# Experts in three blocks, then the second net; x operands in two sets; decode over two blocks

## The chip, the cores and the metric

The program runs on one core of one Trainium2 chip. The metric is the device time of one execution in microseconds; lower is better. Of several executions the median is given.

## The reference, cut to what matters

Three stages follow each other, on 2304 tokens with 512 features, in float32.

```python
# 1. attention inside chunks of 64 tokens, 4 x 8 heads, head size 64
attn = softmax(q_c @ k_c.T / sqrt(64)); x = attn @ v_c           # -> (2304, 512)
# 2. eight experts with weights P from 8 Sinkhorn rounds
P = exp(x @ w_gate - max)
for _ in range(8):
    P /= P.sum(1, keepdims=True) + 1e-9
    P /= P.sum(0, keepdims=True) + 1e-9
    P *= N / E
y = sum(P[:, e:e+1] * (relu(x @ w1[e]) @ w2[e]) for e in range(8))  # 512 -> 1024 -> 512
# 3. the second net: three products, their maximum, one product
h = maximum(maximum(y @ u1, y @ u2), y @ u3)                        # 512 -> 768
out = h @ w_out                                                     # 768 -> 512
```

Stage 3 for a token needs y of that token alone, so a block of tokens can pass to stage 3 as soon as all eight experts are summed for it.

## The kernel before, in words

The tokens are cut into three blocks of 768. A phase is one stage on one block: ("M", b) runs the experts on block b, ("m", b) the second net. An expert phase has 32 items (8 experts, 4 pairs of 128 hidden features each), a phase of the net has 9 (3 pairs of features, 3 products for the maximum). Items are numbered through: before, 0 to 31 and 32 to 63 are the experts on blocks 0 and 1, 64 to 72 the net on block 0, 73 to 104 the experts on block 2, 105 to 113 and 114 to 122 the net on blocks 1 and 2.

An item's up half (`up`, L187) is a Strassen scheme of seven products, so that 7 products replace 8. Each operand is kept as a high and a low part (`xh`, `xl` for x, `wh`, `wl` for weights), and each product is six matmuls of 384 columns on TensorE (L235). Between products ScalarE copies a partial sum out of PSUM (`s`, L240), VectorE adds (L243), and `finish` (L208) makes the hidden operands `hh` and `hl`; in the net it takes the maximum into `m` (L225) first. The down half (`down`, L256) is six matmuls of 512 columns per tile of 128 tokens (L267), six tiles per expert item and six per three items of the net. The down tiles of an item are placed between the products of the following items: after products 0 to 5 of an expert item, or after products 2 and 4 of an item of the net.

The order of the work is written out by hand. The main loop (L712) walks the items and their seven products; `at(n, pos, fn)` (L606) hangs other work behind product `pos` of item `n`. Each engine runs its instructions in that order. All transfers are issued from SP's queue, in that order too.

What hangs there:

- Weights of an item are made in block 0 (`prep`), kept in device memory (`keep`, tensors `w1s`, `w2s`), and loaded again for later blocks: `fetch(n + 1)` behind product 1, `fetch2(n)` at product 2, before the work hung there (L725).
- `y_out` (L305) transposes the summed outputs of an expert phase tile by tile early in the next phase and stores them (`ys`).
- The weights of the second net come as 64-bit floats and are decoded on the chip by `decode_all` (L410): 24 jobs of eight or nine steps, two loads ahead, with integer operations on VectorE, a high part on ScalarE (`dhi`), a low part on POOL (`dlo`), and two stores to `scr` or `scro`. The first step of the next job (L388) writes `scm`, which has the same buffer as `dhi`, and stands in one step with the stores. The steps hang on the second block of experts (L641).
- The x operands of a phase are changed at its start. `x_load` (L329) reads them four and three items ahead, `x_sums` (L339) makes the Strassen differences two items ahead, and `x_put` (L345) writes `xh` and `xl`, one of seven parts behind each product of the last item before the phase, since the matmuls of that item still read them. In the first phase, `x_head` (L349) makes them from the attention in pieces of 128 columns instead.

SBUF tiles come from pools; `big` (opened by `att_close`, L627) holds `m`, the decode's buffers and the tiles of `x_load`.

Of the kernel before, what the change touches and what calls it, by code (L numbers as in the profile page):

```python
# [9 lines left out]
F32 = mybir.dt.float32  # L10
F32R = mybir.dt.float32r
# [7 lines left out]
P = 128  # L19
# [10 lines left out]
KD = DM // P  # L30
SB = 3
TS = NT // SB
W = TS * P // 2
NPAIR = E * F // 256
# [3 lines left out]
NPE = 6  # L38
# [9 lines left out]
def kernel(ctx: ExitStack, tc: tile.TileContext, qk, vv, wg, wts, wts2, out):  # L48
    nc = tc.nc
    pool = lambda name, bufs=1, **kw: ctx.enter_context(tc.tile_pool(name=name, bufs=bufs, **kw))  # L50
    cp = pool("const")
    wp = pool("w", 2)
    hp_ = pool("h", 2)
    tp_ = pool("t", 1)
    raws = ExitStack()
    rp = raws.enter_context(tc.tile_pool(name="raw", bufs=1, side="right"))
    accp = pool("acc")
# [12 lines left out]
    mr = cp.tile([1, P], F32, name="mr")  # L70
    rs = cp.tile([P, NT], F32, name="rs")
    cs = cp.tile([P, E], F32, name="cs")
    cp.tile([P, 480], F32, name="gap")
    xh = cp.tile([P, 7, 2, W], F32R, name="xh")
    xl = cp.tile([P, 7, 2, W], F32R, name="xl")
    xs = dram.tile([NT, P, KD, P], F32, name="xs")
    ys = dram.tile([NT, P, KD, P], F32, name="ys")
# [5 lines left out]
    wts2 = wts2.bitcast(I32)  # L83


    phases = [("M", 0), ("M", 1), ("m", 0), ("M", 2), ("m", 1), ("m", 2)]
    items, first_of = [], []
    for kind, sb in phases:
        first_of.append(len(items))
# [11 lines left out]
    st, sw, wh, wl, w2h, w2l = {}, {}, {}, {}, {}, {}  # L101
# [85 lines left out]
    def up(n):  # L187
        it = items[n]
        bank = {"a": ps_a.tile([P, 512], F32, name="pa", tag="pa"),
                "g": ps_g.tile([P, 512], F32, name="pg", tag="pg"),  # L190
                "b": ps_b.tile([P, 512], F32, name="pb", tag="pb")}
        bank = {k: t[:, :W] for k, t in bank.items()}
        begun = set()
        tiny = lambda nm: tp_.tile([P, W], F32, name=nm, tag=nm)
        m2 = it["kind"] == "m"
        if not m2:
            c = tp_.tile([P, 3, W], F32, name="c", tag="c")
        elif it["i"] == 0:
            mt[0] = big[0].tile([P, 4, W], F32, name="m", tag="big")
            c = mt[0]  # L200
        else:
            c = tp_.tile([P, 3, W], F32, name="c", tag="c")
        if it["down"]:
            hh = hp_.tile([P, 4, W], F32R, name="hh", tag="hh")
            hl = hp_.tile([P, 4, W], F32R, name="hl", tag="hl")
            it["h"] = (hh, hl)

        def finish(q, src):  # L208

            if not m2:  # L210
                nc.scalar.activation(out=hh[:, q], in_=src, func=AF.Relu)  # L211
                if q.start == 0:
                    nc.scalar.activation(out=src, in_=src, func=AF.Relu)  # L213
                    nc.gpsimd.tensor_tensor(out=hl[:, q], in0=src, in1=hh[:, q].bitcast(F32),  # L214
                                            op=ALU.subtract)
                    return
                nc.vector.scalar_tensor_tensor(out=hl[:, q], in0=src, scalar=0.0,  # L217
                                               in1=hh[:, q].bitcast(F32), op0=ALU.max, op1=ALU.subtract)
                return
            m = mt[0]  # L220
            if it["i"] == 0:
                if q.start == 3:
                    nc.scalar.copy(out=m[:, q], in_=src)
                return
            nc.vector.tensor_tensor(out=m[:, q], in0=src, in1=m[:, q], op=ALU.max)  # L225
            if it["i"] == 2:
                hilo(hh[:, q], hl[:, q], m[:, q])

        s = {}
        for pos, (wi, xi, b) in enumerate(PRODUCTS):  # L230
            ps = bank[b]
            for k in range(2):
                ws = slice(k * P, (k + 1) * P)
                for i, (x, y) in enumerate(((wh[n], xh), (wh[n], xl), (wl[n], xh))):
                    nc.tensor.matmul(ps, lhsT=x[:, wi, ws], rhs=y[:, xi, k], start=b not in begun,  # L235
                                     stop=k == 1 and i == 2, skip_group_check=True)
                    begun.add(b)
            if pos < 3:
                s[pos] = tiny(f"s{pos}")
                nc.scalar.copy(out=s[pos], in_=ps)  # L240
            elif pos < 6:
                q, other = {3: (0, 0), 4: (1, 1), 5: (2, 2)}[pos]
                nc.vector.tensor_tensor(out=c[:, q], in0=ps, in1=s[other], op=ALU.add)  # L243
                if pos == 4:
                    finish(slice(0, 2), c[:, 0:2])
                elif pos == 5:
                    finish(slice(2, 3), c[:, 2:3])
            else:
                finish(slice(3, 4), ps.unsqueeze(1))
            yield pos  # L250
# [94 lines left out]
    def x_put(pos):  # L345
        i = PRODUCTS[pos][1]
        hilo(xh[:, i], xl[:, i], xst[i], nc.vector if pos % 2 == 0 else None)

    def x_head(j, r, eng):  # L349

        cols = slice(j * P, (j + 1) * P)
        T = ap_.tile([P, 4, 2, P], F32, name="xT", tag="xT", bufs=1)
        for o, a, b in ((T[:, 0], r[:, 1, 0:2], r[:, 0, 0:2]), (T[:, 1], r[:, 1, 2:4], T[:, 0]),
                        (T[:, 2], r[:, 1, 2:4], r[:, 1, 0:2]), (T[:, 3], r[:, 0, 2:4], T[:, 1])):
            eng.tensor_tensor(out=o, in0=a, in1=b, op=ALU.subtract)
        yield
        raw = r[:, 0].rearrange("p (i k) q -> p i k q", i=2)
        nc.scalar.copy(out=xh[:, 0:2, :, cols], in_=raw)
        nc.scalar.copy(out=xh[:, 2, :, cols], in_=r[:, 1, 2:4])
        nc.gpsimd.tensor_tensor(out=xl[:, 0:2, :, cols], in0=raw, in1=xh[:, 0:2, :, cols].bitcast(F32),  # L360
                                op=ALU.subtract)
        nc.gpsimd.tensor_tensor(out=xl[:, 2, :, cols], in0=r[:, 1, 2:4], in1=xh[:, 2, :, cols].bitcast(F32),
                                op=ALU.subtract)
        for i in range(2):
            c = slice(3 + 2 * i, 5 + 2 * i)
            nc.scalar.copy(out=xh[:, c, :, cols], in_=T[:, 2 * i:2 * i + 2])
        yield
        for i in range(2):
            c = slice(3 + 2 * i, 5 + 2 * i)
            nc.vector.tensor_tensor(out=xl[:, c, :, cols], in0=T[:, 2 * i:2 * i + 2],  # L370
                                    in1=xh[:, c, :, cols].bitcast(F32), op=ALU.subtract)
        yield


    big = [None]

    def decode_load(srcs):
        w = big[0].tile([P, 512, 2], I32, name="w64", tag="ld", bufs=3)
# [72 lines left out]
    ap_ = att.enter_context(tc.tile_pool(name="att", bufs=2))  # L451
    wones = ap_.tile([P, 2 * DM], BF16, name="wones", tag="eT", bufs=1)[:, 0:DM]
    q_t, v_t, s_t, e_t, et_t, at_t, raw_t = {}, {}, {}, {}, {}, {}, {}
# [152 lines left out]
    def at(n, pos, fn):  # L606
        bg.setdefault((n, pos), []).append(fn)
# [18 lines left out]

    def att_close():  # L627
        att.close()
        big[0] = pool("big")

    def raw_close():
        raws.close()
# [5 lines left out]
        for step in range(4):  # L638
            at(g + step // 3, (0, 1, 6, 1)[step], lambda g=g, step=step: keep(g, step))
    dec, folds = decode_all(), fold_all()  # L640
    for a in range(NPAIR + 1, first_of[2] - 1):  # L641
        for b in range(7):
            for _ in range(1 + (b == 3)):
                at(a, b, lambda: next(dec, None))
    at(first_of[2] - 2, 6, lambda: [None for _ in dec])
    f0 = 4 * NRAW + 2
    for i in range(NRAW * TS + 2):
        at(f0 + i // 4, (0, 2, 4, 5)[i % 4], lambda: next(folds, None))
    for k in range(1, len(phases)):
        n0 = first_of[k]  # L650
        g = x_load(k)
        for i in range(13):
            at(n0 - 4 + i // 7, i % 7, lambda g=g: next(g, None))
        for step in range(4):
            at(n0 - 2, step + 2, lambda step=step: x_sums(step))
        for pos in range(7):
            at(n0 - 1, pos, lambda pos=pos: x_put(pos))

    def warm(n):
        p = wk.tile([P, 512], F32, name="warm", tag="wk")  # L660
# [3 lines left out]
    with tc.manual_schedule():  # L664
# [14 lines left out]
        for k in range(NPE + 2):  # L679
            if k < NPE:  # L680
                att_qk(k)
                load_qk(k + 3)
            if k >= 2:
                att_pv(k - 2)
                load_v(k + 1)
            if 1 <= k <= NPE:
                att_norm(k - 1)
            if k < NPE:
                att_exp(k, 2)
            if 1 <= k <= NPE:  # L690
                att_T(k - 1)
            warm(4 if k < NPE else 0)
            if k == 0:
                prep(0, 0)
                raw1(1)
            if k == 1:
                prep(0, 1)
            if k == 3:
                prep(0, 2)
                raw2(1)  # L700
            if xg:
                next(xg.pop(0))
            if k >= 3 and k % 2:
                g = x_head(k // 2 - 1, raw_t[k // 2 - 1], nc.gpsimd if k < NPE else nc.vector)
                next(g)
                next(g)
                xg.append(g)
# [72 lines left out]
```

## Time and profile before

| | us |
|---|---|
| median of 3 runs | 1940.75 (1938.32 to 1941.76) |
| the profiled execution | 1934.4 |
| its span, first to last instruction | 1932.6 |
| TensorE busy with matmuls | 1882.9 |
| VectorE (DVE) busy | 1116.0 |
| ScalarE (ACT) busy | 690.7 |
| GpSimd (POOL) busy | 636.1 |
| mean granted TensorE clock | 0.989 of full speed |

Durations are from one profiled execution, on its own clock. Starts in the trace are counted from the first instruction. The busy times are sums over the span, and matmuls overlap, so a full TensorE row does not tell how close to its best it runs; the times between like places of successive items do. The chain of waits is followed back from the last instruction, and successive matmuls of one destination are one piece in it, with their number behind an x.

### The profile page before, as it was taken

Reading aid. Unit: us, or ns where it says so; the run is one execution under the profiler, and the core shown is the slowest. Engines: PE = TensorE matmul, PEld = TensorE weight load, DVE = VectorE, ACT = ScalarE, POOL = GpSimd, SP = SyncE. Lnnn points to the kernel's source line nnn. Section 1 sums busy time; section 2 is a strip of 40 time slices with the busy share of each in tenths; the row PEclk is TensorE's granted clock in tenths of the full one; section 3 lists DMA queues with packets and bytes.
Section 4 is the critical chain, followed back from the end, with each engine's and each line's share of the span. In section 5 each row is a group of like instructions: output and inputs, shape, how many; then the busy total and the mean of one; then the engine's idle time right before and its main releaser. Section 6 shows DMA issues by size and latency. Waiting matters only on the chain.

```text
span 1932.6 us, 26875 instructions
## 1 busy us (share of the span) xinstructions
PE 1882.9 (97%) x10397; PEld 1681.6 (87%) x10403; DVE 1116.0 (58%) x1748; ACT 690.7 (36%) x1194; POOL 636.1 (33%) x438
## 2 busy tenths in 40 slices
PE   7999999999999999999999999999999999999998
PEld 4988888888888888889888989898989988889897
DVE  7566555637875777677766545444445444453534
ACT  4545554454444333233323332322222222233221
POOL 6666666778872221222221211211111111111201
PEclk8999999999999999999999999999999999999999
DMA  7587967778888766767776457544444444647562
GB/s 252 189 301 265 329 248 278 284 278 297 328 325 300 255 228 235 269 240 253 264 264 226 188 214 259 212 180 179 180 180 180 182 189 191 225 172 253 192 247 93
DMA packets 172673, 455.30 MB, mean 236 GB/s; under 512 B 14465, under 2 KB 81025, under 8 KB 172545
## 3 DMA queue, kind: packets, MB, share of 16 engines
q1 hardware_dynamic: 172544, 453.58, 64.1%
q8 instruction: 82, 1.34, 0.3%
q14 instruction: 47, 0.38, 0.1%
HBM read 319.57 MB, written 132.38 MB: 234 GB/s over the span
## 4 chain that ended last, share of the span: by engine, by line
PE 88%; DVE 4%; DMA 4%; ACT 3%; issue 1%; POOL 1%; SPq 0%; DVEq 0%; ACTq 0%; POOLq 0%
PE dn L267 42%; PE pa L235 24%; PE pg L235 12%; PE pb L235 6%; DMA w2l<-w2s 2%; DMA scr<-dhi 1%; PE s L478 1%; PE gp L569 1%; DVE c L243 1%; PE warm L662 1%; ACT hh L211 1%; PE xp L557 1%; DVE acc L290 1%; DVE xl L182 1%; DVE hl L217 0%
## 5 line engine op out<-in xcount | busy, mean ns | idle before, releaser
L267 PE MATMUL dn<-w2h,hh 128*128 128x512 f32 x1260 | 498.9, 396 | 12.3 <-ACT hh L181 6.0
L267 PE MATMUL dn<-w2h,hl 128*128 128x512 f32 x1260 | 502.8, 399 | 3.7 <-DVE hl L217 3.4
L267 PE MATMUL dn<-w2l,hh 128*128 128x512 f32 x1260 | 499.8, 397 | 2.8 <-DMA w2l<-w2s 2.8
L290 DVE SCALAR_TENSOR_TENSOR acc<-dn,Pt,acc 128x512 f32<-128x512 f32 x438 | 327.1, 747 | 276.2 <-PE dn L267 274.8
L214 POOL TENSOR_TENSOR hl<-c,hh 128x768 fp32r<-128x768 f32 x96 | 177.9, 1853 | 828.3 <-ACT c L213 820.0
L235 PE MATMUL pa<-xh,wh 128*128 128x384 f32 x984 | 333.8, 339 | 8.0 <-ACT s L240 8.0
L235 PE MATMUL pa<-xl,wh 128*128 128x384 f32 x984 | 331.9, 337 | 0.0
L235 PE MATMUL pa<-xh,wl 128*128 128x384 f32 x984 | 330.9, 336 | 0.0
L211 ACT ACTIVATE hh<-c 128x768 fp32r<-128x768 f32 x192 | 131.8, 687 | 451.5 <-DVE c L243 451.2
L267 PEld LDWEIGHTS dn<-w2h,hl 128*128 128x128 f32 x1260 | 237.6, 189 | 59.3 <-DVE hl L217 7.0
L267 PEld LDWEIGHTS dn<-w2h,hh 128*128 128x128 f32 x1260 | 238.6, 189 | 46.4 <-ACT hh L181 6.6
L267 PEld LDWEIGHTS dn<-w2l,hh 128*128 128x128 f32 x1260 | 237.9, 189 | 33.8 <-DMA w2l<-w2s 4.0
L240 ACT COPY s<-pa 128x384 f32<-128x384 f32 x246 | 118.1, 480 | 251.7 <-PE pa L235 251.6
L235 PEld LDWEIGHTS pa<-xh,wh 128*128 128x128 f32 x984 | 185.4, 188 | 23.7 <-ACT s L240 11.1
L235 PEld LDWEIGHTS pa<-xl,wh 128*128 128x128 f32 x984 | 185.3, 188 | 13.2
L235 PEld LDWEIGHTS pa<-xh,wl 128*128 128x128 f32 x984 | 185.3, 188 | 0.0
L235 PE MATMUL pg<-xh,wh 128*128 128x384 f32 x492 | 166.7, 339 | 3.7 <-DVE c L243 3.7
L235 PE MATMUL pg<-xl,wh 128*128 128x384 f32 x492 | 167.1, 340 | 0.0
L235 PE MATMUL pg<-xh,wl 128*128 128x384 f32 x492 | 166.4, 338 | 0.0
L217 DVE SCALAR_TENSOR_TENSOR hl<-c,hh 128x384 fp32r<-128x384 f32 x96 | 109.0, 1135 | 60.6 <-ACT hh L211 59.4
L243 DVE TENSOR_TENSOR c<-pb,s 128x384 f32<-128x384 f32 x114 | 63.1, 554 | 99.2 <-PE pb L235 93.9
L240 ACT COPY s<-pg 128x384 f32<-128x384 f32 x123 | 59.1, 480 | 156.1 <-PE pg L235 155.9
(123 smaller groups left out, 2372.4 us busy)
## 6 DMA issues: line engine op xcount, KB each, us to landing
wh<-w1s SPq DMA_DIRECT2D x64, 896.0 KB, 4.7
wl<-w1s SPq DMA_DIRECT2D x64, 896.0 KB, 6.6
w2h<-w2s SPq DMA_DIRECT2D x64, 512.0 KB, 7.4
w2l<-w2s SPq DMA_DIRECT2D x64, 512.0 KB, 8.2
w1s<-wh SPq DMA_DIRECT2D x32, 896.0 KB, 7.4
w1s<-wl SPq DMA_DIRECT2D x32, 896.0 KB, 9.1
wh<-scr SPq DMA_DIRECT2D x27, 896.0 KB, 4.7
wl<-scr SPq DMA_DIRECT2D x27, 896.0 KB, 6.6
```

The costliest lines, as they stand in the source:

```text
L182: (eng or nc.gpsimd).tensor_tensor(out=l, in0=v, in1=h.bitcast(F32), op=ALU.subtract)
L211: nc.scalar.activation(out=hh[:, q], in_=src, func=AF.Relu)
L214: nc.gpsimd.tensor_tensor(out=hl[:, q], in0=src, in1=hh[:, q].bitcast(F32), op=ALU.subtract)
L217: nc.vector.scalar_tensor_tensor(out=hl[:, q], in0=src, scalar=0.0, in1=hh[:, q].bitcast(F32), op0=ALU.max, op1=ALU.subtract)
L235: nc.tensor.matmul(ps, lhsT=x[:, wi, ws], rhs=y[:, xi, k], start=b not in begun, stop=k == 1 and i == 2, skip_group_check=True)
L240: nc.scalar.copy(out=s[pos], in_=ps)
L243: nc.vector.tensor_tensor(out=c[:, q], in0=ps, in1=s[other], op=ALU.add)
L267: nc.tensor.matmul(p, lhsT=h[:, hi, ts], rhs=w[:, f, :], start=(f == 0 and i == 0), stop=(f == 1 and i == 2))
L290: nc.vector.scalar_tensor_tensor(out=acc[t], in0=p, scalar=Pt[:, t, e:e + 1], in1=acc[t], op0=ALU.mult, op1=ALU.add)
L478: nc.tensor.matmul(ss[g][cs, hp, :], lhsT=a[r, hp, 0, cs], rhs=a[r, hp, 1, cs], start=True, stop=True)
L557: nc.tensor.matmul(p[64 * g:64 * g + 64, hp, :].rearrange("p (a q) -> p a q", a=2), lhsT=v[r, h * D:(h + 1) * D], rhs=aT[r, :, he, :], sta ...
L569: nc.tensor.matmul(p, lhsT=x[:, k, :], rhs=wgr[:, k, :], start=k == 0, stop=k == KD - 1)
```

## The change

The phases are put in the order M0, M1, M2, m0, m1, m2, so items 32 to 95 are experts on blocks 1 and 2 and 96 to 122 the net. `x_head` becomes `x_cols`, with the pool and the destinations as parameters. For the net on blocks 1 and 2 the new generator `x_next` reads `ys` and makes the x operands in three pieces, one step behind products 0, 2, 4 and 6 of the items of the phase before, for block 1 into a second set (`xb`), for block 2 into the first. The second set lies in a pool `big2` that takes the place of `big` after item 95. The decode's steps hang on items 33 to 94, at products 0, 2, 4, 6 of even and 1, 3, 5 of odd items; before, they hang on items 33 to 62 at every product, two at product 3. Two empty tiles change size (`gap`) or are added (`edge`).

```diff
--- before.py
+++ after.py
@@ -52,6 +52,7 @@
     wp = pool("w", 2)
     hp_ = pool("h", 2)
     tp_ = pool("t", 1)
+    pool("edge", side="right").tile([P, 120], F32, name="edge")
     raws = ExitStack()
     rp = raws.enter_context(tc.tile_pool(name="raw", bufs=1, side="right"))
     accp = pool("acc")
@@ -70,7 +71,7 @@
     mr = cp.tile([1, P], F32, name="mr")
     rs = cp.tile([P, NT], F32, name="rs")
     cs = cp.tile([P, E], F32, name="cs")
-    cp.tile([P, 480], F32, name="gap")
+    cp.tile([P, 8], F32, name="gap")
     xh = cp.tile([P, 7, 2, W], F32R, name="xh")
     xl = cp.tile([P, 7, 2, W], F32R, name="xl")
     xs = dram.tile([NT, P, KD, P], F32, name="xs")
@@ -83,7 +84,7 @@
     wts2 = wts2.bitcast(I32)
 
 
-    phases = [("M", 0), ("M", 1), ("m", 0), ("M", 2), ("m", 1), ("m", 2)]
+    phases = [("M", 0), ("M", 1), ("M", 2), ("m", 0), ("m", 1), ("m", 2)]
     items, first_of = [], []
     for kind, sb in phases:
         first_of.append(len(items))
@@ -191,6 +192,7 @@
                 "b": ps_b.tile([P, 512], F32, name="pb", tag="pb")}
         bank = {k: t[:, :W] for k, t in bank.items()}
         begun = set()
+        vh, vl = xb if first_of[4] <= n < first_of[5] else (xh, xl)
         tiny = lambda nm: tp_.tile([P, W], F32, name=nm, tag=nm)
         m2 = it["kind"] == "m"
         if not m2:
@@ -231,7 +233,7 @@
             ps = bank[b]
             for k in range(2):
                 ws = slice(k * P, (k + 1) * P)
-                for i, (x, y) in enumerate(((wh[n], xh), (wh[n], xl), (wl[n], xh))):
+                for i, (x, y) in enumerate(((wh[n], vh), (wh[n], vl), (wl[n], vh))):
                     nc.tensor.matmul(ps, lhsT=x[:, wi, ws], rhs=y[:, xi, k], start=b not in begun,
                                      stop=k == 1 and i == 2, skip_group_check=True)
                     begun.add(b)
@@ -346,10 +348,12 @@
         i = PRODUCTS[pos][1]
         hilo(xh[:, i], xl[:, i], xst[i], nc.vector if pos % 2 == 0 else None)
 
-    def x_head(j, r, eng):
+    xb = []
+
+    def x_cols(j, r, eng, pl, xh, xl):
 
         cols = slice(j * P, (j + 1) * P)
-        T = ap_.tile([P, 4, 2, P], F32, name="xT", tag="xT", bufs=1)
+        T = pl.tile([P, 4, 2, P], F32, name="xT", tag="xT", bufs=1)
         for o, a, b in ((T[:, 0], r[:, 1, 0:2], r[:, 0, 0:2]), (T[:, 1], r[:, 1, 2:4], T[:, 0]),
                         (T[:, 2], r[:, 1, 2:4], r[:, 1, 0:2]), (T[:, 3], r[:, 0, 2:4], T[:, 1])):
             eng.tensor_tensor(out=o, in0=a, in1=b, op=ALU.subtract)
@@ -371,8 +375,25 @@
                                     in1=xh[:, c, :, cols].bitcast(F32), op=ALU.subtract)
         yield
 
-
-    big = [None]
+    def x_next(k):
+
+        for j in range(TS // 2):
+            r = big[0].tile([P, 2, KD, P], F32, name="xr", tag="xr")
+            for q in range(2):
+                nc.sync.dma_start(out=r[:, q], in_=ys[phases[k][1] * TS + 2 * j + q])
+            yield
+            yield
+            yield
+            yield from x_cols(j, r, nc.vector, big[0], *(xb if k == 4 else (xh, xl)))
+
+    def big_again():
+        bigs.close()
+        big[0] = ctx.enter_context(tc.tile_pool(name="big2", bufs=1))
+        big[0].tile([P, 4, W], F32, name="m", tag="big")
+        xb.extend(big[0].tile([P, 7, 2, W], F32R, name=nm) for nm in ("xbh", "xbl"))
+
+
+    big, bigs = [None], ExitStack()
 
     def decode_load(srcs):
         w = big[0].tile([P, 512, 2], I32, name="w64", tag="ld", bufs=3)
@@ -626,7 +647,7 @@
 
     def att_close():
         att.close()
-        big[0] = pool("big")
+        big[0] = bigs.enter_context(tc.tile_pool(name="big", bufs=1))
 
     def raw_close():
         raws.close()
@@ -638,15 +659,14 @@
         for step in range(4):
             at(g + step // 3, (0, 1, 6, 1)[step], lambda g=g, step=step: keep(g, step))
     dec, folds = decode_all(), fold_all()
-    for a in range(NPAIR + 1, first_of[2] - 1):
-        for b in range(7):
-            for _ in range(1 + (b == 3)):
-                at(a, b, lambda: next(dec, None))
-    at(first_of[2] - 2, 6, lambda: [None for _ in dec])
+    for a in range(NPAIR + 1, first_of[3] - 1):
+        for b in range(a % 2, 7, 2):
+            at(a, b, lambda: next(dec, None))
+    at(first_of[3] - 2, 6, lambda: [None for _ in dec])
     f0 = 4 * NRAW + 2
     for i in range(NRAW * TS + 2):
         at(f0 + i // 4, (0, 2, 4, 5)[i % 4], lambda: next(folds, None))
-    for k in range(1, len(phases)):
+    for k in range(1, 4):
         n0 = first_of[k]
         g = x_load(k)
         for i in range(13):
@@ -655,6 +675,12 @@
             at(n0 - 2, step + 2, lambda step=step: x_sums(step))
         for pos in range(7):
             at(n0 - 1, pos, lambda pos=pos: x_put(pos))
+    at(first_of[3] - 1, 6, big_again)
+    for k in (4, 5):
+        g = x_next(k)
+        for a in range(first_of[k - 1] + 1, first_of[k]):
+            for b in range(0, 7, 2):
+                at(a, b, lambda g=g: next(g, None))
 
     def warm(n):
         p = wk.tile([P, 512], F32, name="warm", tag="wk")
@@ -701,7 +727,7 @@
             if xg:
                 next(xg.pop(0))
             if k >= 3 and k % 2:
-                g = x_head(k // 2 - 1, raw_t[k // 2 - 1], nc.gpsimd if k < NPE else nc.vector)
+                g = x_cols(k // 2 - 1, raw_t[k // 2 - 1], nc.gpsimd if k < NPE else nc.vector, ap_, xh, xl)
                 next(g)
                 next(g)
                 xg.append(g)
```

## Rows read from the trace of the kernel before

**Rows 1.** The page, part 4: the chain's share of the span by line

```profile
PE dn L267 42%; PE pa L235 24%; PE pg L235 12%; PE pb L235 6%; DMA w2l<-w2s 2%; DMA scr<-dhi 1%; PE s L478 1%; PE gp L569 1%; DVE c L243 1%; PE warm L662 1%; ACT hh L211 1%; PE xp L557 1%; DVE acc L290 1%; DVE xl L182 1%; DVE hl L217 0%
```

**Rows 2.** Windows: length, busy us of PE, PEld, DVE, ACT, POOL, PEclk, DMA, GB/s

```profile
584.00:1109.00 525.00, 512.53 (x2522) 454.69 (x2521) 353.76 (x618) 176.11 (x292) 112.15 (x60) 0.99 0.69 248
...
1213.00:1715.00 502.00, 501.33 (x2482) 450.23 (x2483) 246.10 (x350) 141.95 (x237) 66.19 (x37) 0.99 0.50 191
```

**Rows 3.** Chain of waits, whole span: start us, length us, what

```profile
569.35 2.08 PE pa L235 x12
...
620.44 2.10 PE pa L235 x12
628.80 3.85 DMA scr<-dhi
...
716.89 2.10 PE pa L235 x12
...
726.59 10.55 DMA w2l<-w2s
...
752.35 2.08 PE pa L235 x12
...
958.68 9.08 DMA w2l<-w2s
...
1094.28 2.08 PE pa L235 x12
...
1156.11 2.09 PE pa L235 x12
1166.19 2.08 PE pa L235 x12
...
1197.54 2.08 PE pa L235 x12
1209.39 2.02 DVE xl L182
1213.67 3.16 PE dn L267 x6
...
1230.31 2.10 PE pa L235 x12
...
1700.12 2.09 PE pa L235 x12
...
1763.50 2.10 PE pa L235 x12
...
1805.07 2.12 PE pa L235 x12
...
1832.36 2.10 PE pa L235 x12
```

**Rows 4.** Groups by line and shape, whole span: busy us, mean ns | idle before

```profile
L370 DVE TENSOR_TENSOR xl<-xT,xh 128x512 fp32r<-128x512 f32 x6 | 8.0, 1360 | 1.8 <-ACT xh L366 1.7
...
L360 POOL TENSOR_TENSOR xl<-xr,xh 128x512 fp32r<-128x512 f32 x3 | 4.9, 1631 | 2.2 <-ACT xh L358 2.2
...
L366 ACT CAST xh<-xT 128x512 fp32r<-128x512 f32 x6 | 3.7, 618 | 6.1 <-POOL xT L355 4.3 <-DVE xT L355 1.7
```

**Rows 5.** Timeline of 1776 to 1790: start us, us, engine, line, operation

```profile
1783.98 1.85 POOL L182 TENSOR_TENSOR hl<-m,hh 128x768 fp32r<-128x768 f32 x1 [27.04 <-issue]
...
1784.45 1.78 DVE L225 TENSOR_TENSOR m<-c,m 128x384 f32<-128x384 f32 x1
```

**Rows 6.** SP's queue, 1290 to 1345, third expert block

```profile
1309.49 0.32 SPq L170 DMA_DIRECT2D wh<-w1s  x1
```

**Rows 7.** SP's queue, 700 to 740, around the start of item 40

```profile
721.97 0.52 SPq L447 DMA_DIRECT2D scr<-dlo  x1
...
724.32 1.27 SPq L170 DMA_DIRECT2D wh<-w1s  x1
```

**Rows 8.** VectorE's groups by shape, 584 to 1109 (second expert block)

```profile
L388 DVE TENSOR_SCALAR scm<-w 128x512 int32<-128x512 int32 x24 | 11.7, 488 | 65.2 <-DMA scr<-dhi 40.9 <-issue 8.3 <-DMA w<-in_wts 7.4
```

## The prediction, made before the change was run

> **What bounds the kernel now.** I read the page first, then the windows by block, then the chain of waits with its start times, then the queue of SP, then the groups by line. The page's chain gives the two matmul lines (L235, L267) 84% of the span [rows 1]. By block TensorE is busy 501.33 of 502 us in the third expert block, which has no decode beside it, and 512.53 of 525 in the second, which has [rows 2]. So only time in which TensorE waits, or runs slow after a wait, can be won; VectorE's load is not a price in itself.
>
> The chain merges the last product of an item and the first of the next into one piece of twelve matmuls of `pa`, so these pieces are item marks, 1.04 us (half of 2.08) before the start of the item. From 1230.31 to 1700.12 lie 30 expert items: 15.66 us each, without a wait. From 1156.11 to 1166.19 lies one item of the second net: 10.08. Anything above these two is loss [rows 3]:
>
> - Decode: 620.44 to 1094.28 are 29 expert items, 473.84 us against 454.14, so 19.7 us lost.
> - Block 0 to block 1: 569.35 to 620.44, three items: 51.09 − 46.98 = 4.1 (the block's y transposes, about as long at every block's end, are in it).
> - Block 1 to net 0: 1094.28 to 1156.11, one expert item and four of the net: 61.83 − 55.98 = 5.85.
> - Net 0 to block 2: 1197.54 to 1230.31: 32.77 − 25.74 = 7.03.
> - Block 2 to net 1: 1700.12 to 1763.50: 63.38 − 55.98 = 7.40.
> - Net 1 to net 2: 1805.07 to 1832.36, two items: 27.29 − 20.16 = 7.13.
> - An ordinary third item of the net to the next first one: 1166.19 to 1197.54, three items: 31.35 − 30.24 = 1.11.
>
> Why net 0 to block 2 costs 7 us can be read there: a VectorE subtract of 2.02 us (`xl`, from x_put) holds the eviction behind it, the down matmuls start at 1213.67, and six of them take 3.16 us, where an undisturbed group takes (15.66 − 7 × 1.04) / 6 = 1.40 [rows 3]. TensorE is at 1.2 instead of 2.4 GHz after such a wait, so a wait costs more than its length.
>
> **Order of the phases and x in two sets.** The handovers before, without block 0 to 1, which stays: 5.85 + 7.03 + 7.40 + 7.13 = 27.4, and two ordinary third-to-first ones within nets 0 and 1, 2.2: together 29.6. After the change there are block 1 to block 2, block 2 to net 0, and, between the nets, items that follow each other as within a net, as no x_put stands there and the x operands are ready earlier. Block 1 to 2 is like block 0 to 1 with decode steps beside it: 4.1 at the least, 7.4 (the costliest of a block's end) at the most; I take 5.1, near the same kind of handover. Block 2 to net 0: the same pair as block 2 to net 1, same place in the rotation of weight buffers, 7.4; at the least 5.85. Between the nets: five ordinary handovers that are not in these figures, 5 × 1.11 = 5.55. Sum 18.05, gain 11.6 us (bounds 9.3 and 14.1).
>
> **x_next in place of x_load, x_sums and x_put, twice.** It runs in chunks of 128 columns, three per phase, one step at every second product of items of a net. One chunk has four ScalarE copies (0.62 us for 512 elements: some 2.3 with the shorter ones), two POOL subtracts (1.63 for 512, some 2.7 both), two VectorE subtracts of 1.36 and four shorter ones [rows 4]. The ScalarE copies stand at product 0 of the third item (twice) and product 4 of a first one. At product 0 they go ahead of the copy of s1, which is wanted only by product 5; s2, wanted by product 4, is ready after 2.3 + 2 × 0.48, and product 4 starts 4 × 1.04 + 1.40 = 5.6 after the item. So they hide behind matmuls, with some two us to spare. If VectorE's four subtracts, issued at product 6 just before, run late, the spare is used up. I take 1 us for all; the cover gone, it is the third rival. On SP's queue: the loads of chunks two and three wait until POOL has read the chunk before and hold up only a weight fetch needed an item later; the first load stands an item ahead of its reader. Six loads of 256 KB replace twelve of half that.
>
> One rule speaks against this part. The trace shows a VectorE max of `m` with 384 elements that takes 1.78 us while a POOL subtract of 1.85 us runs from just before it [rows 5]; that makes the 1.11 us above. The Trainium skill, in SBUF — State Buffer, section Who interferes with whom, says that a VectorE instruction with both inputs in SBUF is blocked by a GpSimd instruction that reads SBUF, for its whole length. The trace agrees here. By that rule alone, six chunks with 2.7 us of POOL could each hold such a VectorE step: 6 × 2.7 = 16 us in place of my 1. I don't take it, since the max stands at products 4 to 6 of second and third items, and the chunks' POOL work at products 0 to 3 of third items or at 4 of a first one, which has no max.
>
> **Decode over two blocks.** The work stays: 24 jobs, 213 steps. What changes is the distance of steps, from one product (two steps at product 3) to two products, 2 × (1.04 + 1.40) = 4.9 us at most. Two mechanisms make the 19.7 us.
>
> First, a fetch held on SP's queue. The weights of an item are fetched when it starts: 1309.49 [rows 6], beside a start of 1230.31 + 5 × 15.66 + 1.05 = 1309.66. In item 40, which starts at 716.89 + 1.04 = 717.93, the store of `dlo`, which waits for POOL, is issued at 721.97 and the fetch only at 724.32 [rows 7], 6.4 us late; `w2l`, issued at 726.59, lands 10.55 later at 737.14, while item 41 wants it at about 734.6. Items 40 and 41 together: 716.89 to 752.35 is 35.46 − 31.32, 4.1 lost [rows 3]. The chain has four such `w2l` pieces (the first and the last are shown); read alike they lost 4.1, 5.2, 1.0 and 1.2, 11.5 in all. A fetch is held where the hi/lo step stands late in one item, or at product 0, and the store at product 0 or 1 of the next steps. Laying the steps out: eight jobs take 70 steps, which is 20 items at 3.5 steps each, so the places repeat every 20 items. The store stands ahead of the fetch in items 44, 64, 84 with the hi/lo step at product 5 of the item before, early enough, and in items 49, 69, 89 with it at product 6, just as in item 40. Of these three the last has no further load behind it. I take two at the mean of the four, 2 × 2.9 = 5.8; between none and 3 × 5.2.
>
> Second, VectorE waits at the first step of the next job until the store of `dhi`, in the same buffer, has landed. L388 has 65.2 us of idle time before 24 instructions, 2.7 each [rows 8]. A store takes 3.85 us on the chain [rows 3]. That leaves 19.7 − 11.5 = 8.2 us of TensorE's time to these waits and the crowded steps behind them. With 4.9 instead of 2.4 us between hi/lo step and next job most of the wait is gone, and behind it stand half as many decode steps per item. It stays where the store queues behind the weight fetch: hi/lo at product 0 or 1, next job at 2 or 3, six jobs. I take 2 of the 8.2, between 0 and 8.2. Decode then loses 7.8 in place of 19.7 (0 to 23.8), a gain of 11.9.
>
> What else moves costs nothing: the pool that is closed and opened anew comes after the last x_put, and its first tile is written three products later; the empty tiles shift addresses only.
>
> **Sum.** 11.6 + 11.9 − 1 = 22.5 us. The profiled execution took 1934.4 us around its span of 1932.6, so the next would take 1911.9. The median of the runs shown is 1940.75, 6.35 above it; taking the difference as unchanged, 1918.
>
> **Rivals.**
> - Decode loses as much as before, since its 24 waits are the same in number: 11.6 − 1 = 10.6, 1930. For it: the store still shares its buffer. Against: the mean wait of 2.7 us is hardly longer than the 2.4 us by which the steps move apart.
> - Decode loses nothing: 11.6 + 19.7 − 1 = 30.3, 1910. For it: by the item marks thirteen of the 24 jobs lost nothing that counts even at the dense rate. Against: items 49 and 69.
> - Slower: x_next's steps get in the way of the net's VectorE and ScalarE chain. Should each chunk cost what the subtract of 2.02 us cost at net 0 to block 2, 7.03, the six cost 42 and the time is 1940.75 − 23.5 + 42, about 1960. It turns slower above some 4.5 us for a chunk (27 us in all). For it: the third items already wait 1.11. Against: VectorE is otherwise idle at the products where the steps stand.
> - The parts cancel: decode stays and x_next costs about 10: 1940.
>
> **Chances.** Forecast 0.55 (its own range 1912 to 1925), decode as before 0.15, decode free 0.17, slower 0.08, cancelling 0.05. The range 1907 to 1933 takes in the best of all bounds (14.1 + 19.7) and reaches past the first rival. No change is within 0.2%, some 3.9 us, which is what a measurement can tell: faster 0.87, same 0.05, slower 0.08.
>
> **What would show it.** Right: item marks 15.66 apart in both decode blocks except at items 49/50 and 69/70; L388's idle time far under 65 us; no `xl` on the chain between nets, and the nets' items in threes of 31.35 through all three nets. Wrong: a wait of TensorE in the items where x_next's steps stand, or many small losses per decode job. The forecast falls if the chain shows `xT` or `xr` between matmuls, or the decode blocks lose over 15 us together.

## The result: 1913.6 us, and the profile after

Median 1913.56 us of 4 runs (1912.69 to 1915.51) against 1939.7 for the kernel before beside it: ratio 0.9866, 95% interval [0.9849, 0.9883]. On a second chip the same two took 1915.95 and 1936.65, ratio 0.9896 [0.9877, 0.9916]. The kernel before scatters more (1929 to 1943 over 41 runs on four chips) than the changed one, and by the medians the gain is 26.1 us on the first chip and 20.7 on the second. The forecast was 1918.

The page's chain and the windows of the two expert blocks that now hold the decode (length, then busy us of PE, PEld, DVE, ACT, POOL, clock, DMA, GB/s), to set beside [rows 1, 2]:

```profile
PE dn L269 42%; PE pa L237 25%; PE pg L237 12%; PE pb L237 6%; DMA scr<-dhi 2%; PE gp L590 1%; PE s L499 1%; PE xp L578 1%; DMA w2l<-w2s 1%; PE warm L688 1%; DVE c L245 0%; DMA w2s<-w2l 0%; DVE acc L292 0%; ACT hh L213 0%; POOL wl L183 0%
```

```profile
622.00:1093.00 471.00, 465.67 (x2310) 415.53 (x2309) 285.24 (x461) 139.66 (x235) 79.18 (x42) 1.00 0.61 220
1132.00:1603.00 471.00, 469.27 (x2336) 420.43 (x2335) 283.42 (x453) 142.25 (x240) 79.88 (x43) 1.00 0.60 220
```

TensorE is busy 465.67 of 471 us in the first of them, and 469.27 of 471 in the second.

The item marks of the changed kernel, from the chain of waits (start us, length us), to set beside [rows 3]:

```profile
622.61 2.08 PE pa L237 x12
...
653.89 2.10 PE pa L237 x12
657.36 9.76 DMA scr<-dhi
687.46 2.08 PE pa L237 x12
...
859.61 2.08 PE pa L237 x12
867.67 10.35 DMA w2l<-w2s
891.65 2.08 PE pa L237 x12
...
1084.37 2.08 PE pa L237 x12
...
1138.85 2.08 PE pa L237 x12
...
1595.51 2.08 PE pa L237 x12
...
1657.20 2.08 PE pa L237 x12
...
1886.32 2.08 PE pa L237 x12
```

Read as in the prediction, but with 15.64 and 10.07 us for an undisturbed item (see the sixth experiment for why they are shorter than 15.66 and 10.08):

| stretch | forecast loss | before | after |
|---|---|---|---|
| decode (before 29 items; after 622.61 to 1084.37 and 1138.85 to 1595.51, 29 each) | 7.8 | 19.7 | 8.2 + 3.1 = 11.3 |
| block 1 to block 2 (1084.37 to 1138.85, three items) | 5.1 | | 54.48 − 46.92 = 7.6 |
| block 2 to net (1595.51 to 1657.20, five items) | 7.4 | 7.4 | 61.69 − 55.92 = 5.8 |
| the other items of the nets (1657.20 to 1886.32, 22 items) | 1.1 at each third | | 229.12 − 221.54 = 7.6, seven third ones at 1.1 |

So the handovers came near the forecast, with an error of 2.5 one way and 1.6 the other. The decode's loss fell by two fifths, but not in the places foreseen: item 36 alone (653.89 to 687.46, two items) lost 33.57 − 31.28 = 2.3, where I had next to nothing, and item 49 (859.61 to 891.65) 0.8, where I had 2.9.

VectorE around item 36, and its first step of a job over the whole span, to set beside [rows 8]:

```profile
659.83 0.75 DVE L292 SCALAR_TENSOR_TENSOR acc<-dn,Pt,acc 128x512 f32<-128x512 f32 x1 [1.68 <-PE dn L269]
667.20 0.43 DVE L409 TENSOR_SCALAR scm<-w 128x512 int32<-128x512 int32 x1 [6.61 <-DMA scr<-dhi]
667.54 0.74 DVE L292 SCALAR_TENSOR_TENSOR acc<-dn,Pt,acc 128x512 f32<-128x512 f32 x1
668.20 0.55 DVE L245 TENSOR_TENSOR c<-pb,s 128x384 f32<-128x384 f32 x1
```

```profile
L409 DVE TENSOR_SCALAR scm<-w 128x512 int32<-128x512 int32 x24 | 11.7, 486 | 46.1 <-DMA scr<-dhi 37.1 <-DMA scro<-dhi 6.2 <-POOL dlo L183 2.6
```

Idle time before that step fell from 65.2 to 46.1 us only. Of the 65.2 us, stores ended 44.3 (`dhi` to `scr` 40.9 [rows 8], to `scro` 3.4); the rest were waits for a load, for POOL and for nothing that the profile shows. In the changed kernel stores end 37.1 + 6.2 = 43.3. So the waits for the stores hardly changed in sum, but the longest grew from 4.8 to 6.9 us. One wait of 6.61 us stops everything VectorE has to do for the item, here an eviction and the sum `c`.

### The profile page after: what moved, and what is told of

Same layout as the page of the kernel before. It is cut to its first block, busy times and chain, and to the rows that moved or that the text cites. A ratio compares the mean times of both kernels' runs of the same rounds, so it can differ in the third digit from the quotient of the medians.

```text
span 1912.3 us, 26868 instructions
## 1 busy us (share of the span) xinstructions
PE 1869.4 (98%) x10397; PEld 1671.6 (87%) x10403; DVE 1126.6 (59%) x1768; ACT 689.2 (36%) x1204; POOL 638.2 (33%) x444
## 4 chain that ended last, share of the span: by engine, by line
PE 89%; DMA 3%; DVE 3%; ACT 2%; POOL 1%; issue 1%; SPq 0%; ACTq 0%; DVEq 0%; POOLq 0%
PE dn L269 42%; PE pa L237 25%; PE pg L237 12%; PE pb L237 6%; DMA scr<-dhi 2%; PE gp L590 1%; PE s L499 1%; PE xp L578 1%; DMA w2l<-w2s 1%; PE warm L688 1%; DVE c L245 0%; DMA w2s<-w2l 0%; DVE acc L292 0%; ACT hh L213 0%; POOL wl L183 0%
## 5 line engine op out<-in xcount | busy, mean ns | idle before, releaser
L237 PE MATMUL pa<-xh,wh 128*128 128x384 f32 x912 | 308.0, 338 | 7.1 <-ACT s L242 4.9
L237 PE MATMUL pa<-xl,wh 128*128 128x384 f32 x912 | 307.0, 337 | 0.0
L237 PE MATMUL pa<-xh,wl 128*128 128x384 f32 x912 | 305.5, 335 | 0.0
L237 PEld LDWEIGHTS pa<-xh,wh 128*128 128x128 f32 x912 | 171.5, 188 | 22.8 <-ACT s L242 6.8
L237 PEld LDWEIGHTS pa<-xl,wh 128*128 128x128 f32 x912 | 171.4, 188 | 13.3
L237 PEld LDWEIGHTS pa<-xh,wl 128*128 128x128 f32 x912 | 171.3, 188 | 0.0
L237 PE MATMUL pg<-xl,wh 128*128 128x384 f32 x456 | 153.8, 337 | 0.0
L237 PE MATMUL pg<-xh,wh 128*128 128x384 f32 x456 | 152.8, 335 | 0.4 <-DVE c L245 0.4
L237 PE MATMUL pg<-xh,wl 128*128 128x384 f32 x456 | 152.9, 335 | 0.0
```

## The experiments

Times are medians; each batch ran beside the kernel before on its chip (1936.65 for the first four, 1935.46 for the next four, 1935.94 for the last two). Item losses come from the marks of each run's own trace.

**1. The changed kernel again** (no edit).

> The changed kernel again, on the chip of the next three, as their base. Theory (the gain is in the handovers and the decode): 26 us under the kernel before, as first timed, with the same losses in the trace: about 11 us in items 33 to 94 away from the handover, 2.3 to 2.6 us in each of items 36, 56, 61 and 76. Rival (those four are chance of one execution): the losses stand in other items.

1915.95. The marks give 2.5, 2.3, 2.6 and 2.5 us in items 36, 56, 61 and 76, as in the first trace, so these places are fixed. The block 2 to net handover, 5.8 in the first trace, was 7.3 here: it changes from execution to execution. Item 49 lost 0.2 here instead of 0.8.

**2. The decode dense again.**

```diff
-    for a in range(NPAIR + 1, first_of[3] - 1):
-        for b in range(a % 2, 7, 2):
-            at(a, b, lambda: next(dec, None))
+    for a in range(NPAIR + 1, first_of[2] - 1):
+        for b in range(7):
+            for _ in range(1 + (b == 3)):
+                at(a, b, lambda: next(dec, None))
```

> The changed kernel with the decode's steps where they were before: items 33 to 62, each product, two at product 3. Theory (spreading halves the decode's loss): 19.7 instead of 11 us lost in the decode, some 9 us slower than the changed kernel, less up to 3 us won at the handover of item 63, which is then free of decode steps. Rival (the decode's loss depends on the number of jobs, not on their distance): within 2 us of the changed kernel.

1920.08, ratio to before 0.9918 [0.99, 0.9936]; 4.1 us slower than the changed kernel. Its chain:

```profile
623.68 2.08 PE pa L237 x12
...
1096.65 2.08 PE pa L237 x12
...
1147.70 2.08 PE pa L237 x12
```

Items 34 to 62 lose 472.97 − 453.56 = 19.4, as before the change; the handover to block 2 loses 51.05 − 46.92 = 4.1 instead of 7.6. Both parts of the theory hold: spreading is worth 8.1 us in the items and costs 3.4 of them at the handover, where decode steps then stand beside x_put (the ninth experiment takes them away). What is left of the spreading, 4.1 us by the medians, is a fifth or less of the whole gain.

**3. One set of x operands, x_load for every phase.**

```diff
-    for k in range(1, 4):
+    for k in range(1, len(phases)):
         n0 = first_of[k]
         g = x_load(k)
...
-        vh, vl = xb if first_of[4] <= n < first_of[5] else (xh, xl)
+        vh, vl = xh, xl
```

(with `big_again` and `x_next` left out)

> The changed kernel with x_load, x_sums and x_put for the net on blocks 1 and 2 too, one set of x operands, no second pool; order of phases and decode as changed. Theory (two handovers of some 7 us become ordinary ones of 1.1): 2 x 6 = 12 us slower than the changed kernel, the two losses at items 104 and 105 and 113 and 114. Rival (the order of the phases alone saves the handovers): within 3 us.

1926.76, ratio 0.995 [0.9934, 0.9966]; 10.8 us slower than the changed kernel. The handover from net 0 to net 1 in its chain, two items:

```profile
1696.05 2.08 PE pa L237 x12
1707.91 2.01 DVE xl L183
1723.04 2.08 PE pa L237 x12
```

26.99 − 20.14 = 6.9 us, with the `xl` subtract of x_put between the marks as at the handovers before [rows 3]; the next handover loses 8.1 by the same reading. The order of the phases alone doesn't give the gain between the nets; x operands made ahead do.

**4. A buffer of its own for `scm`, in the changed kernel.**

```diff
-        scm = big[0].tile([P, 2, 512], I32, name="scm", tag="dhi")
+        scm = big[0].tile([P, 2, 512], I32, name="scm", tag="scm")
```

> The changed kernel with a buffer of its own for scm, so that VectorE's first step of a job doesn't wait for the store of the job before. Theory (the 2.3 to 2.6 us in items 36, 56, 61, 76 are that wait): the four go, 9 to 10 us faster than the changed kernel, idle time before the first step (46 us now) under 10. Rival (the loss is crowding of VectorE and the queue of transfers): under 4 us faster.

1904.58, ratio 0.9838 [0.9818, 0.9859]; 11.4 us faster than the changed kernel. Its groups by line, and its chain:

```profile
L409 DVE TENSOR_SCALAR scm<-w 128x512 int32<-128x512 int32 x24 | 16.5, 688 | 0.0
```

```profile
620.99 2.08 PE pa L237 x12
...
863.65 10.07 DMA w2l<-w2s
...
1075.06 2.08 PE pa L237 x12
...
1129.68 2.08 PE pa L237 x12
...
1583.73 2.08 PE pa L237 x12
```

The gain is a little over the 9 to 10 us of the theory. Idle time before L409 is gone, and the items lose 454.07 − 453.56 = 0.5 and 454.05 − 453.56 = 0.5, one held fetch each (items 49 and 69). So of the 11.3 us that the decode still costs the changed kernel, 10.3 are this wait and 1.0 held fetches. The handover from block 1 to block 2 still loses 54.62 − 46.92 = 7.7 us here (1075.06 to 1129.68), so its loss is not this wait.

**5. The kernel before again, one execution.**

> The kernel before once more, for a second profile: its profiled execution took 1934.4 us, its timed ones 1938 to 1942. Theory (fetches held behind the decode's stores cost more or less by how the transfers meet): a time near 1939 with more loss in items 40, 43, 53 and 54 than the 11.5 us of the first profile. Rival: the same losses there, the difference outside the second expert block.

1939.38, of which its trace shows a little more loss in the decode (items 34 to 62: 476.36 − 454.14 = 22.2 instead of 19.7) and a later start of the items (the mark of item 34 is at 623.52 instead of 620.44, in the same kernel):

```profile
623.52 2.10 PE pa L235 x12
...
729.29 11.31 DMA w2l<-w2s
...
1099.88 2.08 PE pa L235 x12
```

Both theories hold in part: by the starts of the items in the trace the four places lost 13.9 us instead of 11.5, and the other 3.1 us lie ahead of item 34. The program of the opening is the same in all kernels here and its end moved by 3 us from execution to execution.

**6. The two empty tiles alone, in the kernel before.**

```diff
+    pool("edge", side="right").tile([P, 120], F32, name="edge")
...
-    cp.tile([P, 480], F32, name="gap")
+    cp.tile([P, 8], F32, name="gap")
```

> The kernel before with the sizes of the two empty tiles alone as in the changed one (gap 8, edge added), so that tiles lie at other addresses. Expert items with n mod 3 of 1 or 2 took 15.67 us before and 15.64 after. Theory (that is the address): 1 to 3 us faster than before, all items at 15.64. Rival (it came with the order of items): no change, 15.67 stays.

1929.89, ratio 0.9972 [0.996, 0.9985]: faster, by 3 to 8 us. Its third expert block:

```profile
1229.44 2.08 PE pa L236 x12
...
1698.64 2.08 PE pa L236 x12
1760.38 2.08 PE pa L236 x12
```

30 items in 469.20 us, 15.64 each, against 15.66 [rows 3]. Over the 62 expert items of blocks 1 and 2 and the 27 items of the nets (all plain ones at 10.07, where those of nets 1 and 2 took 10.10 to 10.15) that makes some 2 us. The remainder of the measured difference, some 3.6 us by the medians, lies in the decode and in the handover into net 1. Both scatter; but that handover lost 7.3 to 7.4 in all three traces with the old sizes (before, 5 and 8), and 5.8 in six of nine with the new ones (7.3 in 1 and 4), so some of it may come from the sizes too, which is not shown. For the item times it was the address, and not the order.

**7. A buffer of its own for `scm`, in the kernel before** (edits of 4 and 6).

> The kernel before with e6's tiles and a buffer of its own for scm. Theory (of the 19.7 us lost in the second expert block some 8 are VectorE's waits for the store, 11.5 held fetches): 8 us faster than e6, with losses only in items 40, 43, 53, 54. Rival (held fetches are a result of the same wait): nearly all of the 19.7 goes.

1924.29, ratio 0.9941 [0.9927, 0.9955]; 5.6 us faster than 6, where the theory had 8.

```profile
623.65 2.08 PE pa L236 x12
...
727.33 9.16 DMA w2l<-w2s
...
776.21 10.87 DMA w2l<-w2s
...
936.87 10.53 DMA w2l<-w2s
...
1087.58 2.08 PE pa L236 x12
```

463.93 − 453.56 = 10.4 us lost, all in items 40, 43 and 53 (1.4, 5.1 and 3.9); 6 lost 18.7. So by the marks the wait for the store was worth 8.4 before the change, and held fetches the rest, near the 8.2 and 11.5 of the prediction. The medians differ by less; the trace of this run reaches item 34 at 623.65, that of 6 at 621.06, so in that execution 2.6 us of the 8.4 were lost again ahead of the decode.

**8. The down weights' fetch first, in the kernel before.**

```diff
+                if pos == 0:
+                    fetch2(n)
                 if pos < 2:
                     prep(n + 1, pos)
                 elif pos == 2 and n:
                     prep(n, 2)
-                    fetch2(n)
```

> The kernel before with the fetch of an item's down weights issued ahead of everything hung on its product 0, in place of product 2. Theory (a store of the decode holds SP's queue and so this fetch): the losses in items 40, 43, 53, 54 go, 11 us or more faster than before. Rival (the fetch is late because the transfers are slow): under 3 us.

1926.94, ratio 0.9958 [0.9944, 0.9973]; 8.5 us faster than before.

```profile
620.86 2.10 PE pa L235 x12
...
717.07 2.10 PE pa L235 x12
732.76 2.10 PE pa L235 x12
...
813.82 2.10 PE pa L235 x12
...
924.82 2.10 PE pa L235 x12
...
1007.90 2.10 PE pa L235 x12
...
1086.36 2.08 PE pa L235 x12
```

465.50 − 454.14 = 11.4 lost instead of 19.7 and 22.2. No `w2l` piece is left on its chain, and item 40 (717.07 to 732.76) loses nothing, nor does item 41: there the fetch was late because SP's queue held it. But 8.3 to 10.8 us are won in the decode, not the 11 or more of the theory. Items 41 to 45 still lose 81.06 − 78.30 = 2.8, and items 53 to 57 lose 83.08 − 78.30 = 4.8, where they lost 5.3 before (932.21 to 1015.81): with the held fetches gone there, VectorE's waits for the store take most of their place. Experiment 7 shows the reverse, 3.9 us in item 53 alone. So the two losses are separate in cause, but do not add up exactly.

**9. Three edits on the changed kernel:** those of 4 and 8, and no decode steps in items 63 and 64.

```diff
-        for b in range(a % 2, 7, 2):
+        for b in range(7) if a < NPAIR + 3 else () if a in (63, 64) else range(a % 2, 7, 2):
```

> The changed kernel with three edits: scm in a buffer of its own (e4), the fetch of an item's down weights ahead of the work hung on product 0 (e8), and no decode steps in items 63 and 64 (the seven slots lost stand in items 33 and 34). Theory (the handover from block 1 to block 2 lost 7.6 us instead of 4.1 because decode steps stood beside x_put): 4.1 to 4.3 us at items 63 and 64, nothing in items 49 and 69, 4 us faster than e4, near 1900. Rival (the third block's first items are slow for another reason): the handover stays over 7 us, 1 us faster than e4.

1899.86, ratio 0.9819 [0.9799, 0.9839]. The handover from block 1 to block 2, three items:

```profile
1077.35 2.08 PE pa L237 x12
...
1128.42 2.08 PE pa L237 x12
```

51.07 − 46.92 = 4.15, and every other item of blocks 1 and 2 takes 15.64: the decode now costs nothing. The three edits stand in one run; that it is the decode's steps that the handover paid for follows from this run and 2, which both lose 4.1 without them, and 4, which loses 7.7 with them.

**10. In addition, another order of `hl` in the nets.**

```diff
-                hilo(hh[:, q], hl[:, q], m[:, q])
+                nc.scalar.copy(out=hh[:, q], in_=m[:, q])
+                for r in {0: (), 2: (slice(1, 3),), 3: (slice(3, 4), slice(0, 1))}[q.start]:
+                    nc.gpsimd.tensor_tensor(out=hl[:, r], in0=m[:, r], in1=hh[:, r].bitcast(F32),
+                                            op=ALU.subtract)
```

> e9, and in the third items of the net POOL makes hl of parts 1 and 2 after product 5 and of parts 3 and 0 after product 6, instead of 0 and 1 after product 4, 2 after 5 and 3 after 6, so that no POOL subtract runs while VectorE takes the maximum of c and m for part 2. Theory (the 1.1 us at each ordinary handover within the net is VectorE held by POOL): eight handovers go to under 0.3, some 7 us faster than e9. Rival (ScalarE's copies of hh before s0 are the delay, whenever they start): the 1.1 us stays, or the late hl holds the down matmuls and it is slower.

1891.37, ratio 0.9773 [0.9753, 0.9793]; 8.5 us faster than 9 and the fastest of all. VectorE and POOL at the end of a third item, from the timelines of the two engines, and item marks in the chain:

```profile
1782.43 0.56 DVE L227 TENSOR_TENSOR m<-c,m 128x384 f32<-128x384 f32 x1
```

```profile
1783.67 3.79 POOL L231 TENSOR_TENSOR hl<-m,hh 128x768 fp32r<-128x768 f32 x3 [26.41 <-issue]
```

```profile
1640.80 2.08 PE pa L240 x12
...
1842.13 2.08 PE pa L240 x12
```

The maximum that took 1.78 us behind POOL [rows 5] takes 0.56 when POOL starts after it, and 20 items of the nets, six of them the first after a third one, take 201.33 us, 10.07 each. The 1.1 us is gone.

## Why the prediction was right, and where it was not

**Right: what bounds the kernel.** TensorE's item times were the floor, and nearly every microsecond that a run won or lost lies in a stretch where the marks are further apart than that. The exceptions are the floor itself, which the empty tiles moved (6), and the start of item 34, which scatters by 3 us.

**Right: the handovers.** Forecast gain 11.6; by the marks 29.6 before against 7.6 + 5.8 + 5 × 1.1 = 18.9, a gain of 10.7. Two sizes were off. Block 1 to block 2 was put at 5.1 with 7.4 as the most; it is 7.6. The step "near the same kind of handover" held only without decode beside it (4.1 in 2 and 9). In the changed kernel decode subtracts stand in front of x_put's chain, and the one of L124 takes 1.82 us, where L123 and L125 beside it take 0.28; POOL's `xl` subtract runs from 1094.70 for 1.89 us:

```profile
1094.91 1.82 DVE V L124
...
1100.84 1.98 DVE xl L183
```

Block 2 to net was put at 7.4, and took 5.8 in the first trace and 7.3 in the second of the same kernel; what decides between the two was not found.

**Right: x_next is hidden.** Put at 1 us; the items of the nets with its steps take 10.07 us and the third ones lose 1.1, like those of the last net, which has none. The rule on VectorE and GpSimd would have made it 16. The Trainium skill's sentence (SBUF — State Buffer, Who interferes with whom) is right on the lock, and experiment 10 shows it. Here too the trace agrees: x_next's own VectorE subtracts (L374) take up to 1.22 us beside its POOL subtracts, and 0.68 at the least. But no other VectorE instruction with both inputs in SBUF runs beside those, and the items with these steps take no longer than those of the last net, so the lock costs nothing there.

**Near in sum, wrong in its parts: the decode.** Forecast 7.8, measured 11.3. The step that failed: "With 4.9 instead of 2.4 us between hi/lo step and next job most of the wait is gone ... I take 2 of the 8.2". It is 10.3 (4), more than before the change. I had named the condition, that the store queues behind the weight fetch, and mis-sized it; I had also taken all of the 65.2 us for the wait on `dhi`, where 40.9 were [rows 8]. In item 36 the store of `dhi` is issued at 657.36, after the four fetches of the item on the same queue, and lands 9.76 us later; at 628.80 in the kernel before, 6.1 us behind the last fetch, it took 3.85 [rows 3], and with no fetch close ahead 3.0 to 3.4. In the dense order no store of `dhi` followed the last fetch of an item by less than 4.9 us, and some went ahead of the fetch, which then came late itself (item 40 [rows 7]). In the new order the fetch goes first, by 1.3 to 3.7 us in nine of the 24 jobs, the store behind it takes 6.2 to 10.0 us, and VectorE pays instead. The idle time fell (65.2 to 46.1 us), but four waits, three of 6.6 to 6.9 us and one of 4.5 (item 61), cost TensorE 2.3 to 2.6 each, since evictions stand behind them. A sum over mean waits could not show that. The Trainium skill (DMA: Bandwidth & Descriptors, Queues, rings and completion order) says that each DMA engine takes up the descriptors of a ring in ring order; the trace agrees, with 9.76 behind the fetch against 3.0 to 3.4 without one.

The other half, held fetches, was put at 5.8 and is 1.0. In item 49, which starts at 859.61 + 1.04, `w2l` is issued at 867.67 and lands at 878.02; it is wanted at 860.65 + 15.64 + 1.04 = 877.33. In item 40 before it came 2.5 us late, here 0.7; item 69 lost 0.3. A loss that begins only at a threshold can't be priced by the mean of four cases that passed it by different lengths.

**Wrong: "the empty tiles shift addresses only", at no cost.** They are worth some 2 us by the items' times and 3 to 8 by the medians (6), so a tenth of the gain at the least. Which of the moved tiles matters was not tried.

**The base.** I added 6.35 us to the profile's sum, as the difference of the median to the profiled execution. The changed kernel's profiled execution took 1914.13, its median 1913.56. The sum itself, 1911.9, was 2.2 us under that execution. The kernel before has medians of 1935 to 1940 by the chip, and its profiled execution happened to be a quick one: a second one (5) took 1939.38.

**How much of it was luck.** That 1918 came within 4.4 us is in part luck. The waits for the store cost 8.3 us more than forecast and the held fetches 4.8 less; the handovers gained 0.9 less, x_next cost 1 less, and the empty tiles gave 2 that were not in the sum. Of the signs named, two failed: four items outside 49, 50, 69 and 70 lost over 2 us, and L388's idle time (L409 in the changed kernel) stayed at 46.1. The others held: no `xl`, `xT` or `xr` on the chain between the nets, threes of 31.3 us there, and under 15 us lost in the decode.

A reader of the code should also know that from item 32 on the up weights loaded behind product 1 of item n are those of item n + 2, not n + 1; the steps above hang on `w2l`, for which the text ahead is right.

## What to carry to other kernels

Where one engine is the floor, measure like places of successive items: every loss shows as a distance, and its item number leads to the instruction. A wait that is moved off one queue can come back on another: when stores and loads share a queue, spreading the work decides who is in front, and a buffer shared between a step and a pending store makes the engine that runs the step wait for the store. Give such a step its own buffer first, then spread.

## What the runs showed of the hardware that was not expected

Moving tiles by 1.9 KB or less per partition changed an item of TensorE-bound work from 15.66 to 15.64 us, and items of the net from up to 10.15 to 10.07, in all nine traces with the new sizes against all three with the old ones. The opening of the program, the same in all kernels, ended up to 3 us later from one execution to the next. In the kernel before, TensorE stood still from 1209.7 to 1213.67 at the handover from net 0 to block 2 [rows 3]; the granted clock was 1.00 ahead of that and 0.50, that is 1.2 GHz, from 1213.60 to 1217.00, and six down matmuls took 3.16 instead of 1.40 us there. In the last kernel, with the waits gone, the granted clock is 1.00 throughout 622 to 1075, 1127 to 1579 and 1641 to 1843, its blocks 1 and 2 and the nets away from the handovers.
